# One-hot operands of the routing in tiles of their own, and a new order of issue

## The chip, the cores and the metric

The kernel runs on one core of a Trainium2 chip. The metric is the time on the device of one execution, in microseconds (us), as the median of three runs. One further execution was profiled, and its trace is what is read here.

## The reference, cut to what matters

```python
# 1. attention with random features: 4 batches, 8 heads, 576 tokens, 64 wide, 128 features
q_p, k_p = phi(q_s), phi(k_s)                 # exp(x @ omega.T - ... - rowmax) / sqrt(m)
kv = einsum('bhsm,bhsd->bhmd', k_p, v);  z = sum(k_p, axis=2)
num = einsum('bhsm,bhmd->bhsd', q_p, kv)
den = einsum('bhsm,bhm->bhs', q_p, z)[..., None] + 1e-06
x = num / den                                 # 2304 tokens of 512
# 2. dense layer
h = x @ w_in                                  # 512 -> 1024
solu = h * softmax(h)
x = layernorm(solu) * g_ln @ w_out            # 1024 -> 512
# 3. one expert of 8 for each token
logits = x @ w_gate;  e_idx = argmax(logits);  gate_w = softmax(logits)[e_idx]
eom = sigmoid(x @ w_output_gate)
for e in range(8):
    out[mask] = gate_w[mask] * eom[mask, e] * (relu(x[mask] @ w1[e]) @ w2[e])
```

## The kernel before, in words

The 2304 tokens are 18 tiles of 128. Everything up to the routing is cut into named steps, and one list, ORDER, says in which order they are issued: `kp7` is step `kp` for tile 7. Each engine issues its own instructions strictly in the order of that list; a second list, LOADS, is the order of the loads on SP's queue. A load waits there until the buffer that it takes over is free: `k` and `q` share six, `v` has three.

The steps of a tile: `kp`, `kx`, `ke` (TensorE, VectorE, ScalarE) make the key features, `kv` adds them into a batch's sums; `vc`, `vt`, `vd`, `vz`, `vy` carry a finished batch's sums into SBUF tiles `kv` and `zb` by way of `kt` and `zk`. `qp`, `qx`, `qe` make the query features, `qz` (GpSimd, tile `pz`), `qr` (VectorE, tile `rd`) and `qs` (GpSimd) divide, `qta`, `qtb` transpose, `qca`, `qcb` copy and `nx` gives the attention's output, which `xh` and `xl` split into a rounded and a remaining part. `ha`, `hb` are the first dense product in two halves, `hxa`, `hxb`, `he`, `ma`, `mz`, `mb`, `mc`, `md`, `me` the activation and the norm, `ta`, `tb`, `ca`, `cb`, `sa`, `sb` its transposed parts `lth` and `ltl`, and `u`, `l` the second product, 24 products of 256 or 272 columns each, with the logits beside `u`; `ua`, `ub`, `la` take the results out of PSUM and `lo` stores them. `da` to `dl`, `ga` to `gd` turn the weights into two parts (chunks 0 to 7 for the first product, 8 to 15 for the second). `wu7` is seven products that are thrown away.

Routing: tiles come in sets, 0 to 3, 4 to 7, 8 to 11, 12 to 14, 15 and 16, and 17. `ra`, `rb`, `rc`, `rd`, `re`, `rf` work out where each token of a set goes. `rg` makes the one-hot operands `ea` and `er` of a tile on VectorE, and `rh` multiplies them into the table `tab`. `za` finds the largest expert, `zl` and `zm` load its weights into `raw1` and `raw2` through SP, and `wa`, `wb` split two quarters of the first; the other two quarters are split in hooks of the first unit and stand in no list. `zb` and `zg` gather the expert's first 256 tokens from tiles 0 to 14, `zt` transposes them, `zh` and `zs` split them into `xteh` and `xtel`.

After the list comes the first unit: `up` makes eight chunks of hidden features from 256 columns, `hth` on ScalarE and `htl` on VectorE, with hooks between the chunks, for the last set (`rest`) and for `raw2`, and `down` follows, in which `first_item` adds the rest of the table and fetches the remaining tokens of the item; `up` then runs at column 256 with 336 columns. From there on the items follow one another.

SBUF: `ab` and `rt` are pools that live through this part, `att` is the attention's; it is closed at `zl0`, and the pool `c1` with `raw1` and `raw2` takes its place. PSUM has eight banks: four in `big`, two in `sm`, two in `kvp` (`tab` and `places` at last); `psh` and `psy` take over those of `big`.

## Time and profile before

| | us |
|---|---|
| three runs, median (lowest to highest) | 609.11 (607.41 to 609.7) |
| the profiled execution | 607.34 |
| its span, from the first to the last instruction | 605.7 |
| TensorE busy | 587.7 |
| VectorE busy | 356.7 |
| ScalarE busy | 298.1 |
| GpSimd busy | 261.0 |

Busy times are unions, so a matmul that starts while another is under way is not counted twice; matmuls are pipelined, and a busy TensorE may still be waiting between them. PE is TensorE's matmul, PEld its weight load, DVE VectorE, ACT ScalarE, POOL GpSimd, SP the queue that issues most loads. TensorE's granted clock was 0.998 of full speed over the span.

### The profile page before, as it was taken

To read this page: it belongs to the slowest core of one execution; us is meant where nothing else is said; L and a number is where in the kernel's file an instruction comes from. 1 tells how busy PE (TensorE), PEld (TensorE's weight loads), DVE (VectorE), ACT (ScalarE), POOL (GpSimd) and SP (SyncE) were. 2 spreads that over 40 slices of the span, in tenths; PEclk is the share of its full clock that TensorE was granted. 3 is DMA by queue.
4 is the path that set the end of the run, shared out by engine and by line. 5 is a ranking of instruction groups with operands and counts; after the bars stand their busy time and mean duration, and the time that the engine had idled before them with its cause. 6 is when DMAs were issued, how large, how long until landed. Compare 5 with 4: busy or idle time off the path is not lost. (4 is left out here: it accounts for less than half of the span.)

```text
span 605.7 us, 12756 instructions
## 1 busy us (share of the span) xinstructions
PE 587.7 (97%) x5022; PEld 519.6 (86%) x5022; DVE 356.7 (59%) x960; ACT 298.1 (49%) x746; POOL 261.0 (43%) x283
## 2 busy tenths in 40 slices
...
GB/s 320 364 238 171 176 67 77 99 1 86 38 53 19 2 19 18 18 19 1 18 20 202 128 58 64 30 111 300 264 140 26 165 109 140 35 36 11 2 52 30
DMA packets 21721, 56.45 MB, mean 93 GB/s; under 512 B 2596, under 2 KB 3004, under 8 KB 21652
## 3 DMA queue, kind: packets, MB, share of 16 engines
...
q14 instruction: 27, 0.22, 0.1%
q10 hardware_dynamic: 288, 0.13, 0.1%
...
## 5 line engine op out<-in xcount | busy, mean ns | idle before, releaser
L164 PE MATMUL x<-w2h,lth 128*128 128x272 f32 (+1 forms) x288 | 83.4, 290 | 0.0
L164 PE MATMUL x<-w2h,ltl 128*128 128x272 f32 (+1 forms) x288 | 82.1, 285 | 0.6 <-DVE ltl L152 0.6
L164 PE MATMUL x<-w2l,lth 128*128 128x272 f32 (+1 forms) x288 | 81.9, 284 | 0.0
L982 DVE SCALAR_TENSOR_TENSOR htl<-hp,hth 128x296 fp32r<-128x296 f32 (+2 forms) x64 | 29.8, 466 | 75.0 <-ACT hth L981 61.1
L498 POOL TENSOR_TENSOR pz<-qe,zb 128x256 f32<-128x256 f32 (+1 forms) x80 | 62.6, 813 | 19.9 <-ACT qe L391 12.0
L164 PE MATMUL hp<-xth,w1h 128*128 128x296 f32 (+1 forms) x224 | 67.6, 302 | 0.6 <-DVE htl L982 0.6
L164 PE MATMUL hp<-xth,w1l 128*128 128x296 f32 (+1 forms) x224 | 67.7, 302 | 0.0
L164 PE MATMUL hp<-xtl,w1h 128*128 128x296 f32 (+1 forms) x224 | 67.2, 300 | 0.0
L164 PE MATMUL yp<-w2h,hth 128*128 128x512 f32 (+2 forms) x168 | 65.5, 390 | 0.0
L164 PE MATMUL yp<-w2l,hth 128*128 128x512 f32 (+2 forms) x168 | 64.4, 383 | 0.0
L164 PE MATMUL yp<-w2h,htl 128*128 128x512 f32 (+2 forms) x168 | 64.3, 383 | 0.0
L164 PE MATMUL h<-w1h,xth 128*128 128x512 f32 x144 | 59.1, 410 | 0.2
L981 ACT ACTIVATE hth<-hp 128x296 fp32r<-128x296 f32 (+2 forms) x64 | 26.7, 418 | 64.2 <-PE hp L164 63.1
L152 DVE TENSOR_TENSOR xtl<-xT,xth 128x512 fp32r<-128x512 f32 (+1 forms) x36 | 23.9, 665 | 58.1 <-ACT xth L885 42.1
L164 PE MATMUL h<-w1l,xth 128*128 128x512 f32 x144 | 57.1, 396 | 0.3 <-DVE w1l L152 0.3
L600 POOL TENSOR_SCALAR s<-s,st 128x1024 f32<-128x1024 f32 x18 | 21.7, 1206 | 82.4 <-DVE st L596 52.9
L164 PE MATMUL h<-w1h,xtl 128*128 128x512 f32 x144 | 57.0, 396 | 0.0
L164 PEld LDWEIGHTS x<-w2h,ltl 128*128 128x128 f32 x288 | 54.2, 188 | 0.9 <-DVE ltl L152 0.9
L164 PEld LDWEIGHTS x<-w2h,lth 128*128 128x128 f32 x288 | 54.2, 188 | 0.7 <-issue 0.2
L164 PEld LDWEIGHTS x<-w2l,lth 128*128 128x128 f32 x288 | 54.3, 188 | 0.5
L1007 POOL DMA_INDIRECT out_y<-y,idxs x20 | 20.1, 1003 | 77.3 <-ACT y L1006 69.6
L512 POOL TENSOR_TENSOR qe<-qe,rd 128x256 f32<-128x256 f32 x72 | 44.1, 644 | 9.2 <-DVE rd L505 9.2
...
## 6 DMA issues: line engine op xcount, KB each, us to landing
raw<-in_w POOLq DMA_DIRECT2D x12, 1024.0 KB
...
raw<-in_w SPq DMA_DIRECT2D x4, 1024.0 KB, 5.6
```

The costliest lines, as they stand in the source:

```text
L152: return eng.tensor_tensor(out=out_, in0=a, in1=hi.bitcast(F32), op=ALU.subtract)
L164: return in_turn(nc.tensor.matmul(ps, **kw))
L498: nc.gpsimd.tensor_tensor(out=pz[r0:r1, hs], in0=of["qe", t][r0:r1, hs], in1=of["zb", b][r0:r1, hs], op=ALU.mult)
L512: nc.gpsimd.tensor_tensor(out=e3[:, hs], in0=e3[:, hs], in1=rd[:, hs].to_broadcast([P, HS, M]), op=ALU.mult)
L600: nc.gpsimd.tensor_scalar(out=s, in0=s, scalar1=st[:, 10:11], scalar2=st[:, 11:12], op0=ALU.mult, op1=ALU.add)
L981: act = nc.scalar.activation(out=hi, in_=ps[:, 0:n], func=AF.Relu)
L982: dve = nc.vector.scalar_tensor_tensor(out=lo, in0=ps[:, 0:n], scalar=0.0, in1=hi.bitcast(F32), op0=ALU.max, op1=ALU.subtract)
L1007: nc.gpsimd.indirect_dma_start(out=out, out_offset=bass.IndirectOffsetOnAxis(ap=idxs[0:k, col:col + 1], axis=0), in_=y, in_offset=None, bo ...
```

## The change

- `ea` and `er` no longer borrow the buffers of `ft` (two) and `df` (four) of the attention's pool, or the pool `c1` after it closed. They have tiles of their own: `ea` two buffers, `er` one buffer in `rt` for tiles 0 to 14; for tiles 15 to 17 both have two in `c1`.
- `kv`, `pz` and `rd` move from the attention's pool to `ab`; `zk` holds one batch at a time, in one buffer, instead of all four.
- `rg15` and `rg16` leave the list. They are issued on VectorE after the first unit's first `htl`, and `rest` after its second; the splits of `raw2` come two chunks later.
- `zt` takes its bank from `big` instead of `sm`.
- `up` uses the banks of `kvp` beside those of `psh` also for the first item's second part.
- LOADS and ORDER are new. The same steps stand in ORDER, but for `rg15`, `rg16` and the `wu`, which sum to 33 instead of 30.

`issue_after` makes the instructions of its block that run on the same engine follow the given one in that engine's queue.

```diff
 LOADS = [(x[0], int(x[1:])) for x in """
-    k8 w9 k3 w10 k6 k0 v0 w2 c0 k1 v1 w1 w6 k2 v2 k10 k4 c1 q1 k7 w5 w0 v3 k5 q0 w11 v4 k9 w3 k11 v5 k12 v7 w4 v8 k13
-    w8 v6 q2 w7 v10 k15 q5 v9 k14 v11 q4 q6 v12 q13 v13 w15 q8 v15 k17 v14 q16 k16 v16 v17 q3 q10 w14 q7 w13 w12 q9
-    q14 q15 q11 q12 q17
+    k0 w10 k1 w9 k8 c0 k2 w2 w1 k6 v0 k4 v1 q0 k10 k3 w6 k5 v3 v2 w5 w0 k7 v4 c1 w4 q1 v7 v5 w11 v6 k9 q5 v8 k11 q2 v9
+    w3 v10 v11 k12 k15 k13 k17 q8 v13 w8 k14 v12 q3 w7 q4 k16 v14 v15 q16 v16 q12 w15 q7 w14 v17 q6 q13 w12 w13 q9 q11
+    q17 q10 q15 q14
 """.split()]
 ORDER = """
-    da9 wu7 kp8 kx8 ke8 wu3 kp3 db9 dc9 dd9 wu6 kp0 kx3 de9 df9 da10 db10 ke3 wu7 kp1 da2 dc10 kx0 ke0 dd10 de10 df10
-    kx1 dp9 dg9 wu2 ga1 gb1 dh9 wu3 kp6 kv0 da1 dp10 db1 ke1 kx6 dc1 db2 dc2 ke6 dl9 wu2 kp2 kx2 dg10 da6 ga2 gb2 dd2
-    dd1 gc1 ke2 de2 df2 dh10 db6 kv1 kp4 kx4 dc6 dp2 dh2 dl10 kv2 ke4 dd6 kp5 kx5 zc0 kv3 da11 de6 kp10 ke5 kx10 de1
-    df1 db11 dp1 kv4 vc0 qp1 qx1 ke10 qe1 kw4 qp0 dl2 dc11 kv5 dh1 df6 dp6 qx0 qe0 kp7 dd11 da5 dl1 gc2 gx2 de11 df11
-    kx7 db5 dc5 vz0 vy0 dh6 kv6 ke7 dd5 de5 da7 kp9 kx9 dp11 ke9 dl6 qz0 qr0 kv7 kv8 gx1 dg11 df5 vt0 dh11 dl11 vc1
...
-    gb6 qe8 qs6 nx7 xh7 md1 me1 md0 qp9 qx9 mz5 ha4 xh3 qe9 xl3 dc13 dd13 de12 df12 qta6 de13 gy7 mb5 gd7 xl7 hb4 qca6
-    qtb6 ta5 qcb6 dh14 ca5 hxa4 hxb4 dp12 dg12 gc6 df13 gx6 he4 nx6 xh6 sa5 dh12 ga4 gy6 gd6 ma4 ha3 dp13 dg13 ga5 mz2
-    dh8 dh13 tb5 mb2 xl6 gb4 gb5 hxa3 gc4 gx4 gc5 gx5 dl8 dl12 ta2 ca2 sa2 gy5 gy4 gd4 vc3 cb5 vz3 hb3 dl13 gd5 hxb3
-    qz8 dl14 u0 qr8 mc2 me0 sb5 he3 ma3 tb2 l0 cb2 mc5 md5 qs8 sb2 vy3 qta8 mz3 ub0 qtb8 mz4 qp11 qx11 qca8 qcb8 qp10
...
-    md10 me10 mb12 mc12 rg5 sb10 u10 l10 mb13 ub10 ra2 rc2 he16 ma16 rb2 re2 mz16 ua10 rh4 za0 qtb17 zl0 rg6 rh5 qcb17
-    tb14 nx17 ha15 hb15 rg7 xh17 rd2 xl17 ha17 cb14 sb14 hxa15 u14 me14 lo9 hxb15 he15 la10 ma15 rf2 mz15 ub14 lo10
-    mb15 rh6 mb16 md12 mc15 ta13 ca13 tb13 cb13 sa13 sb13 ta12 ca12 sa12 l14 ua14 la14 ta15 rh7 ca15 hb17 rg8 rh8 wa0
-    sa15 wa1 hxa17 mc16 hxb17 he17 ma17 mz17 ta16 ca16 mc13 md13 lo14 rg10 zm0 u13 me13 ub13 tb15 tb12 cb12 sa16 cb15
-    tb16 ua13 cb16 mb17 me12 sb12 u12 ub12 ua12 l13 ra3 ta17 rb3 tb17 la13 rg9 rh9 rc3 rd3 l12 la12 rf3 sb16 ca17 u16
-    mc17 re3 md15 me15 md16 lo12 me16 lo13 rh10 wb0 cb17 sb17 sb15 u15 rg11 rh11 ub16 rg12 sa17 md17 rh12 rg13 ub15
-    ua16 wb1 ua15 l15 ra4 rc4 l16 rd4 la15 lo15 rh13 rg14 rh14 zb0 rf4 zg1 zg0 rb4 u17 me17 la16 lo16 re4 ub17 ra5 l17
-    ua17 rg16 la17 rg15 zt0 zt1 zh0 zh1 zs0 zs1 lo17
+    da10 wu7 kp0 kx0 ke0 da9 db10 dc10 dd10 wu3 kp1 kx1 db9 ke1 wu6 kp8 kx8 ke8 dc9 de10 df10 dp10 da2 wu6 kp2 kx2 ke2
+    wu4 kp6 dd9 kv0 kx6 ke6 db2 de9 dc2 kp4 da1 wu4 kp3 kv1 df9 kx4 ke4 dd2 dg10 kx3 db1 dc1 de2 df2 dp9 dg9 ke3 kp5
+    kx5 dh9 wu2 ga2 gb2 dd1 dl9 de1 dh10 df1 kv2 kp10 dl10 kx10 ke5 wu1 ga1 dp2 dh2 dl2 kv3 kv4 da6 db6 da5 db5 dc6
+    gb1 qp0 dc5 dd6 da4 vc0 de6 df6 ke10 dp1 dh1 gc1 qx0 kw4 kv5 qe0 db4 dc4 gc2 dd5 gx2 dl1 de5 kp7 dp6 dh6 kx7 vz0
+    vy0 dl6 zc0 da0 db0 qp1 ke7 qx1 qe1 da11 df5 qz0 kv6 kv7 qr0 kp9 vt0 vd0 dc0 kx9 dp5 dd0 qp5 gy2 qs0 qx5 gx1 ke9
+    qe5 db11 kv8 vc1 vz1 kp11 qta0 qca0 dd4 de0 df0 dp0 qtb0 qcb0 qp2 dc11 kx11 dd11 de11 ke11 dh0 qx2 nx0 vy1 qe2
...
+    gc0 gx7 qs7 gx0 he5 ma5 tb0 cb0 nx3 sb0 qta7 qca7 xh3 xl3 gy0 ga6 gb6 qp9 qx9 da13 db13 qtb7 vz2 dc13 dd13 qcb7
+    ha4 qe9 dl8 qs6 qta6 qca6 de13 df13 gd0 hxa4 dh15 qtb6 qcb6 gy7 gd7 da12 qp8 qx8 qe8 vc3 dp13 dg13 db12 dc12 mz2
+    nx7 dd12 de12 vy2 vz3 dl15 nx6 xh6 xl6 hb4 hxb4 mb2 xh7 xl7 dh14 ga5 gb5 dl14 mc2 ha3 hb3 df12 he4 gc6 gx6 gc5 gx5
+    qz8 ma4 ha6 hxa3 hxb3 he3 dp12 qr8 gy5 dg12 dh13 ma3 ga4 dh12 dl12 ta2 tb2 gb4 me1 qs8 qta8 gd5 gy6 gc4 ca2 sa2
...
+    lo8 ub8 nx15 nx17 xh17 rh5 xl17 hb16 cb10 sb10 rg6 rh6 md12 hxb16 xh15 tb13 xl15 mb14 cb13 sb13 me10 mc14 me12 rg7
+    he16 ma16 mz16 mb16 ta12 u10 ub10 ra2 ua10 rc2 rd2 rf2 ca12 ta14 tb14 l10 ca14 cb14 sa14 la10 sb14 ha15 hxa15 hb15
+    hxb15 ta16 mc16 rb2 md16 rh7 mc13 md13 l14 he15 ma15 me13 tb12 re2 za0 lo10 ha17 mz15 u14 sa12 rg8 rh8 rg9 md14
+    zl0 ca16 hxa17 cb12 sb12 me14 ub14 ua14 la14 lo14 hb17 hxb17 he17 u13 ua13 ma17 mz17 sa16 mb15 ta15 mc15 rh9 rg10
+    ca15 md15 u12 tb16 rh10 ub13 mb17 tb15 l13 ub12 ra3 rb3 mc17 sa15 ua12 cb15 sb15 rg11 md17 me17 la13 zm0 ta17 rc3
+    rd3 rf3 re3 wa0 me15 cb16 sb16 rh11 l12 la12 u15 me16 rg12 rh12 lo13 ub15 rg13 wa1 tb17 ca17 cb17 sb17 sa17 ua15
+    u16 ub16 ra4 lo12 rh13 l15 ua16 rg14 rh14 zb0 wb0 rc4 l16 la15 rd4 zg1 zg0 lo15 wb1 la16 rb4 u17 re4 rf4 ub17 ua17
+    ra5 l17 la17 zt0 lo17 zt1 zh0 zs0 zh1 lo16 zs1
 """.split()]
@@ -352,8 +352,7 @@
 
 
 
-        kvs = ap.tile([P, B, H, D], F32, name="kv")
-        zk = ap.tile([P, B, 2, M], F32, name="zk")
+        kvs = pool.tile([P, B, H, D], F32, name="kv")
         raws = {}
 
         def load_tok(kind, t):
@@ -452,10 +451,11 @@
 
 
         def vc(b):
+            zk = of["zk", b] = ap.tile([P, 2, M], F32, tag="zk", name=f"zk{b}", bufs=1)
             kt = of["kt", b] = ap.tile([P, 2, 2 * M], F32, tag="kt", name=f"kt{b}", bufs=1)
             for g, ps in enumerate(kv_ps.pop(b)):
                 nc.scalar.copy(out=kt[:, g, :], in_=ps[:, 0:2 * M])
-                nc.scalar.copy(out=zk[:, b, g, :], in_=ps[:, 2 * M:3 * M])
+                nc.scalar.copy(out=zk[:, g, :], in_=ps[:, 2 * M:3 * M])
 
         def vt(b):
             kt, pss = of.pop(("kt", b)), []
@@ -473,13 +473,14 @@
 
 
         def vz(b):
+            zk = of.pop(("zk", b))
             if b:
-                nc.sync.dma_start(out=zd[b - 1:b].rearrange("o (g i m) -> (o i) g m", g=2, i=4), in_=zk[0:P:32, b])
+                nc.sync.dma_start(out=zd[b - 1:b].rearrange("o (g i m) -> (o i) g m", g=2, i=4), in_=zk[0:P:32])
                 return
             of["zp", b] = pss = [half_bank(f"zp{b}_{n}").rearrange("p (i g m) -> p i g m", i=2, g=2) for n in range(2)]
             for i in (0, 2, 1, 3):
                 rows = slice(i // 2 * D, i // 2 * D + D)
-                mm(pss[i // 2][:, i % 2], lhsT=ident[rows, 32 * i:32 * i + 1].to_broadcast([D, P]), rhs=zk[rows, b], start=True, stop=True)
+                mm(pss[i // 2][:, i % 2], lhsT=ident[rows, 32 * i:32 * i + 1].to_broadcast([D, P]), rhs=zk[rows], start=True, stop=True)
 
         def vy(b):
             zb = of["zb", b] = ap.tile([P, H, M], F32, tag="zb", name=f"zb{b}", bufs=2)
@@ -491,14 +492,14 @@
 
 
         def qz(t):
-            pz = of["pz", t] = ap.tile([P, H, M], F32, tag="pz", name=f"pz{t}", bufs=1)
+            pz = of["pz", t] = pool.tile([P, H, M], F32, tag="pz", name=f"pz{t}", bufs=1)
             for b, r0, r1, _, _ in segments(t):
                 for h in range(0, H, HS):
                     hs = slice(h, h + HS)
                     nc.gpsimd.tensor_tensor(out=pz[r0:r1, hs], in0=of["qe", t][r0:r1, hs], in1=of["zb", b][r0:r1, hs], op=ALU.mult)
 
         def qr(t):
-            rd = of["rd", t] = ap.tile([P, H, 1], F32, tag="rd", name=f"rd{t}", bufs=2)
+            rd = of["rd", t] = pool.tile([P, H, 1], F32, tag="rd", name=f"rd{t}", bufs=2)
             r2 = rd[:, :, 0]
             nc.vector.reduce_sum(out=r2, in_=of.pop(("pz", t)), axis=AX.X)
             nc.vector.tensor_scalar(out=r2, in0=r2, scalar1=1e-6 * M, scalar2=None, op0=ALU.add)
@@ -694,7 +695,6 @@
                 V.memset(keep[n], 1.0)
                 V.memset(keep[n][:, :, 0:1], 0.0)
 
-        hp, EA, ER = ap, ("ft", 2), ("df", DF)
         count = [None]
         d0, e0 = r("d0", [P, E]), r("e0", [P, 1])
         first = {}
@@ -810,9 +810,9 @@
 
             i = next(i for i, (a, z) in enumerate(SETS) if a <= t < z)
             k, d = t - SETS[i][0], of["r", i]
-            ea = hp.tile([P, 512], F32R, tag=EA[0], name=f"ea{t}", bufs=EA[1])[:, 0:P]
+            ea = (cx if t >= TA else rt).tile([P, P], F32R, tag="ea", name=f"ea{t}", bufs=2)
             V.tensor_scalar(out=ea, in0=row[:, 0:P], scalar1=d["flo"][:, k:k + 1], scalar2=None, op0=ALU.is_equal)
-            er = hp.tile([P, 512], F32R, tag=ER[0], name=f"er{t}", bufs=ER[1])[:, 0:3 * NR].rearrange("p (i n) -> p i n", i=3)
+            er = (cx if t >= TA else rt).tile([P, 3, NR], F32R, tag="er", name=f"er{t}", bufs=2 if t >= TA else 1)
             V.scalar_tensor_tensor(out=er, in0=row.unsqueeze(1).to_broadcast([P, 3, NR]), scalar=d["col"][:, k:k + 1],
                                    in1=tsc[:, t, :].unsqueeze(2).to_broadcast([P, 3, NR]), op0=ALU.is_equal, op1=ALU.mult)
             of["hot", t] = ea, er
@@ -905,7 +905,7 @@
             gather(first["xge"], j, idxe[:, j:j + 1], TA * P)
 
         def zt(j):
-            ps = of["xTe", j] = sm.tile([P, NPAIR, P], F32, tag="sm", name=f"xTe_{j}")
+            ps = of["xTe", j] = half_bank(f"xTe_{j}").rearrange("p (c m) -> p c m", c=NPAIR)
             for c in range(NPAIR):
                 transpose(ps[:, c, :], first["xge"][:, j, c * P:(c + 1) * P])
 
@@ -947,14 +947,13 @@
                      za=za, zc=zc, wu=warm, zl=zl, zm=zm, zb=zb, zg=zg, zt=zt, zh=zh, zs=zs, wa=wa, wb=wb, wc=wc)
         in_order(begin, 0)
         for what in ORDER:
-            if not first and (what == "zl0" or what.startswith("rg") and int(what[2:]) >= TE):
+            if not first and (what == "zl0" or what.startswith("rg") and int(what[2:]) >= TA):
                 att.close()
                 cx = ctx.enter_context(tc.tile_pool(name="c1", bufs=1, side="right", reuse_waits="tile"))
                 raw1 = first["raw1"] = cx.tile([P, NPAIR, EF], F32, name="raw1")
                 raw2 = first["raw2"] = cx.tile([P, EF // P, DM], F32, name="raw2")
                 first["xge"] = cx.tile([P, CA, DM], F32, name="xge")
                 xte = first["xte"] = [cx.tile([P, NPAIR, CA * P], F32R, name=f"xte{k}") for k in "hl"]
-                hp, EA, ER = cx, ("ea", 2), ("er", 2)
             name = what.rstrip("0123456789")
             in_order(steps[name], int(what[len(name):]))
             if what == f"vc{B - 1}":
@@ -970,7 +969,7 @@
     def up(i, xt, ht, at, n, between={}):
 
         for f in range(EF // P):
-            more = i and f % 4 > 1
+            more = (i or at) and f % 4 > 1
             ps = (kvp if more else psh).tile([P, 512], F32, tag=f"kv{f % 2}" if more else "psh", name=f"hp{i}_{f}_{at}")
             for hook in between.get(f, ()):
                 hook()
@@ -1026,9 +1025,16 @@
     last = []
     got = cp.tile([P, 3, NR], F32, name="got")
     V.tensor_copy(out=got, in_=table)
-    hooks = {2: [lambda: rest(len(SETS) - 1)], 4: [lambda: [rh(t) for t in range(TA, TA + 2)]]}
+    
+    def behind(*steps):
+        with tc.issue_after(done_up[1]):
+            for step in steps:
+                step()
+
+    hooks = {1: [lambda: behind(lambda: rg(TA), lambda: rg(TA + 1))], 2: [lambda: behind(lambda: rest(len(SETS) - 1))],
+             4: [lambda: [rh(t) for t in range(TA, TA + 2)]]}
     for c in range(4):
-        hooks.setdefault(1 + c, []).append(lambda c=c: split_behind(raw2, w2h, w2l, (c,), ()))
+        hooks.setdefault(3+c, []).append(lambda c=c: split_behind(raw2, w2h, w2l, (c,), ()))
     for c in (2, 3):
         hooks.setdefault(c - 2, []).insert(0, lambda c=c: split_expert(raw1, w1h, w1l, (c,), ()))
     up(0, xte, ht, 0, CA * P, hooks)
```

## Rows read from the trace of the kernel before

**Rows 1.** The page: busy us, share of the span, instructions

```profile
PE 587.7 (97%) x5022; PEld 519.6 (86%) x5022; DVE 356.7 (59%) x960; ACT 298.1 (49%) x746; POOL 261.0 (43%) x283
```

**Rows 2.** Windows, all engines: busy us and instructions in each stretch

```profile
core 0: us, PE busy (x) PEld busy (x) DVE busy (x) ACT busy (x) POOL busy (x), PEclk, DMA share, GB/s
...
0.00:10.00 10.00, 8.75 (x68) 8.00 (x70) 4.18 (x10) 5.07 (x13) 0.19 (x4) 1.00 0.78 279
...
10.00:150.00 140.00, 135.22 (x1947) 111.87 (x1945) 134.34 (x281) 114.19 (x348) 96.55 (x104) 1.00 0.45 150
...
150.00:360.00 210.00, 208.18 (x1587) 189.81 (x1587) 136.73 (x451) 99.46 (x249) 76.00 (x108) 1.00 0.13 45
...
360.00:380.00 20.00, 17.61 (x138) 16.34 (x137) 15.90 (x72) 8.22 (x16) 2.89 (x3) 1.00 0.21 67
...
460.00:470.00 10.00, 10.00 (x44) 8.10 (x44) 3.50 (x3) 3.74 (x6) 5.34 (x4) 1.00 0.22 61
...
590.00:605.70 15.70, 8.47 (x61) 7.66 (x59) 0.00 (x0) 1.63 (x3) 1.90 (x2) 0.91 0.12 41
```

**Rows 3.** Timeline of TensorE: start, us; in brackets idle before and its releaser

```profile
368.56 1.21 PE L168 MATMUL xTe<-ident,xge 128*128 128x128 f32 x8
...
370.44 0.38 PE L164 MATMUL hp<-xteh,w1h 128*128 128x256 f32 x1 [0.68 <-ACT xteh L913]
...
372.53 0.38 PE L164 MATMUL hp<-xtel,w1h 128*128 128x256 f32 x1 [1.70 <-DVE xtel L152]
```

**Rows 4.** Timeline of VectorE, the last 9 us before `xtel` is done

```profile
362.28 0.17 DVE L842 TENSOR_TENSOR pick<-tab,d 128x16 f32<-128x16 f32 x1 [1.48 <-PE tab L164]
...
368.40 0.17 DVE L724 TENSOR_TENSOR oh<-desc,em 128x8 f32<-128x8 f32 x1
...
369.19 0.16 DVE L798 TENSOR_REDUCE gw<-dl 128x1 f32<-128x8 f32 x1 [0.62 <-ACT dl L753]
...
370.35 0.71 DVE L816 SCALAR_TENSOR_TENSOR er<-nums,col,tsc 128x480 fp32r<-128x480 f32 x1
...
371.20 1.28 DVE L152 TENSOR_TENSOR xtel<-xTe,xteh 128x512 fp32r<-128x512 f32 x2
```

**Rows 5.** Timeline of ScalarE, the same stretch

```profile
369.22 1.17 ACT L913 CAST xteh<-xTe 128x512 fp32r<-128x512 f32 x2
```

**Rows 6.** Timeline of VectorE in the first unit

```profile
374.54 0.43 DVE L982 SCALAR_TENSOR_TENSOR htl<-hp,hth 128x256 fp32r<-128x256 f32 x1 [0.17 <-ACT hth L981]
...
375.49 1.23 DVE L152 TENSOR_TENSOR w2l<-raw,w2h 128x1024 fp32r<-128x1024 f32 x1 [0.53 <-ACT w2h L155]
...
384.18 0.72 DVE L816 SCALAR_TENSOR_TENSOR er<-nums,col,tsc 128x480 fp32r<-128x480 f32 x1
...
387.15 0.66 DVE L1052 TENSOR_TENSOR got<-got,tab 128x480 f32<-128x480 f32 x1 [0.76 <-PE tab L164]
```

**Rows 7.** Windows, products of `x` alone: columns as in rows 2, without POOL

```profile
362.60:368.40 5.80, 5.80 (x48) 5.74 (x48) 0.23 (x1) 0.47 (x1) 1.00 0.46 136
```

**Rows 8.** Timeline of TensorE in the first item

```profile
386.73 0.38 PE L164 MATMUL tab<-er,ea 128*128 128x480 f32 x1
...
402.31 0.42 PE L164 MATMUL hp<-xth,w1h 128*128 128x336 f32 x1 [0.58 <-DVE htl L982]
```

**Rows 9.** Groups by line on VectorE: busy us, mean ns of one

```profile
L152 DVE TENSOR_TENSOR w2l<-f,w2h 128x512 fp32r<-128x512 f32 x8 | 7.1, 899 | 0.0
...
L152 DVE TENSOR_TENSOR ltl<-lT,lth 128x512 fp32r<-128x512 f32 x36 | 23.7, 681 | 14.2 <-ACT lth L628 14.2
```

**Rows 10.** Timeline of SP in the head

```profile
36.71 0.33 SPq L364 DMA_DIRECT2D v<-in_v  x1
```

**Rows 11.** Timeline of TensorE in the head

```profile
41.65 0.64 PE L164 MATMUL kv<-ke,v 128*32 128x128 f32 x16 [1.61 <-DMA v<-in_v]
```

**Rows 12.** DMA issues: KB each, median us to landing

```profile
raw<-in_w SPq DMA_DIRECT2D x4, 1024.0 KB, 5.6
```

**Rows 13.** Windows, the 70 us before the hand-over, columns as in rows 2

```profile
298.00:368.00 70.00, 68.90 (x514) 64.77 (x513) 51.77 (x209) 31.44 (x68) 16.29 (x20) 1.00 0.28 98
```

More of the change, by code (lines that the diff above doesn't have):

```diff
@@ L96 @@
-    mb3 ua0 la0 md2 qz9 qr9 l1 qe11 qz11 ta3 qx10 qs9 me2 qr11 qs11 u1 ub1 ua1 ha6 ca3 sa3 u2 qe10 ub2 qta11 qz10 qr10
-    mc3 md3 la1 lo1 ua2 tb3 cb3 qca11 qtb11 qcb11 mb4 mc4 sb3 l2 la2 lo2 me3 qp12 qx12 qe12 nx8 xh8 lo0 hxa6 hb6 hxb6
-    he6 qta9 ma6 xl8 qtb9 u3 qca9 qcb9 qz12 mz6 ta4 ca4 sa4 ua3 ub3 qp14 qx14 nx11 qe14 nx9 xh9 ra0 qp16 qx16 rc0 xl9
-    ha7 mb6 qe16 hb7 rb0 tb4 xh11 cb4 hxa7 hxb7 he7 l3 ha8 qs10 la3 lo3 ma7 mz7 mc6 sb4 qta10 qtb10 hb8 qca10 qcb10
-    re0 mb7 ta7 mc7 tb7 ca7 cb7 nx10 qr12 qs12 sa7 sb7 rd0 ha9 xh10 hb9 xl10 hxa8 qz14 hxb8 he8 hxa9 me5 xl11 u5 qr14
```

42 lines of the change are left out of this document (23 added, 19 removed).

## The prediction

> **What bounds the kernel now.** I read the page first, then the windows, then TensorE's waits, then the timelines of the two places that the change touches. The page has TensorE busy in 97% of the span [rows 1]: 587.7 of 605.7 us, 18 idle. The windows say where the idle time lies [rows 2]: 1.3 us in the first 10, 4.8 from 10 to 150, 1.8 from 150 to 360, 2.4 from 360 to 380, and 7.2 in the last stretch, where the last rows are scattered, which the change leaves alone. So a new order of the same products can take back idle time in two places: the head, and the hand-over from routing to the first expert.
>
> In the head "busy" hides waiting. From 10 to 150 VectorE is busy 134.3 of 140 us, while weight loads fill 111.9; from 150 to 360 VectorE falls to 65% and weight loads rise to 90% [rows 2]. The head goes at VectorE's pace, and what counts there is how much VectorE work a list puts ahead of the product that waits for it. The Trainium skill ("Trainium Kernel Development and Optimization", Performance Expectations) calls matmul busy time a bad measure of how near the limit a kernel is and wants LDWEIGHTS busy share instead. By busy time a better list could win 4.8 us from 10 to 150; by that rule's measure the 28 us without a weight load there. The windows side with the rule, and the second rival below goes past what idle time alone allows.
>
> TensorE's own waits are short: 1.61 us for a `v` [rows 11], 0.68 for `xteh` and 1.70 for `xtel` [rows 3], 0.58 for an `htl` [rows 8].
>
> **Hand-over.** After the last product of tile 17 the eight transposes of `xTe` run from 368.56 to 369.77; one product starts at 370.44, after ScalarE's `xteh`, and the next at 372.53, after VectorE's `xtel` [rows 3]. VectorE had waited 0.62 us for an exponential of the last set, then made `ea` and `er` of tiles 15 and 16 (`rg15`, `rg16`: 369.33 to about 370.98) and three small steps of the last set, and only at 371.20 the two `xtel` [rows 4]. ScalarE's two `xteh` were done at 369.22 + 1.17 = 370.39 [rows 5]. The change takes `rg15`, `rg16` and the last set's steps from VectorE's queue ahead of `zs0`, and gives `zt` a bank of its own, so `zt1` no longer waits for `la17`. What is late next is ScalarE: the second `xteh` at 370.3 to 370.4, then one more `xtel` at 0.64 (half of 1.28), so TensorE resumes at 371.0 instead of 372.53: **-1.5**. Bounds: the new list puts both `wb` (1.23 us for a like quarter [rows 6]) behind `zb0`, where VectorE's chain `zb0`, `rf4`, `re4`, `ub17`, `ra5` was just in time; against it stand `l16`, `u17` and `l17`, 24 products each at 5.80/48 = 0.121 us [rows 7], 8.7 us. The chain took from 362.28 to 368.57 [rows 4], 6.3, and with 2.4 more 8.7: a tie, and up to one `wb` may be lost. So -1.6 to -0.3.
>
> **First unit of the expert.** What left VectorE's queue comes back here. Before, from the end of `xtel` (372.48) to the end of `er` of tile 17 (384.90) passed 12.4 us [rows 4, 6]; `rh17` stood on TensorE at 386.73 [rows 8], 14.2 us after the resumption, and VectorE then idled 0.76 for it. Now VectorE may not begin `rg15` before the first `htl`, which started 2.06 us after `xtel` ended, nor the last set before the second. It takes in 1.65 more (`rg15`, `rg16`), and some 1.4 of small steps that filled the wait ahead of that `htl` come later; 0.7 of its idle time goes, as the quarters of `w2l` start two chunks later. That is 14.8, or 13.6 if one `w2l` (1.22) falls behind `er`, against 14.2: 0.6 early to 0.6 late. Queued behind are the `htl`, for whose bank TensorE waits two chunks later. I take **+0.4**; bounds 0 and +3.0, the latter if all four `w2l` come first and the two `w1l` quarters that are in no list (2.44) fall here as well, since `raw1` now loads later: 14.8 + 2.4 - 14.2.
>
> **Second half of the first item.** `up` now uses four banks in place of two for it. TensorE's wait for `htl` at 402.31 was 0.58 [rows 8]; a third chunk no longer needs the first chunk's `htl`. **-0.6**, between 0 and twice that; the two banks held `tab` and `places`, read last at 387.15 [rows 6], long before.
>
> **Head: new lists.** I compare the two lists at `qta8`, in both near the last product that VectorE's total holds up. Ahead of its `qr8` the old list has, and the new one has not, `dl12`, `dl13`, `sa2`, `sa5`, three `gd`, `mz5` and `md0`: 2 x 0.90 + 2 x 0.68 [rows 9], and fourteen short ones near 0.16 [rows 4], together 5.4 us of VectorE. Ahead of `qta8` it also has on TensorE `u0`, `l0` (2.9 each) and 1.5 of short turns; the new one has `ha6`, 12 products of 512 columns at 10/44 = 0.227 [rows 2], 2.7. So the product comes 5.4 earlier and leaves 4.6 more to do: -0.8 at best, 0 at worst, since other products wait too: **-0.3**. Three more units of `wu` (66 instructions for 60) fall where TensorE waits anyway; with no wait there they would cost 6 x 0.11 = 0.7.
>
> The loads share SP's queue, where a `v` waits for one of three buffers. Before, `v6` was issued at 36.71, once `kv5` was done, and `kv6` stood until 41.65 [rows 10, 11]. The new LOADS puts `v7` (which needs `kv3` done) in front of `v5`, and `v8` behind `kv7`: two tight places again, as `v6` and `v9` were. VectorE was busy through it, so 0.
>
> **At nothing.** `kvs`, `pz` and `rd` below the attention's pool and `zk` for one batch at a time: same instructions; `vc` waits for the `vz` before it, several tiles earlier. `zl0` comes later on SP, some 19 us of products, and holds back the stores queued behind; a `raw` load landed 5.6 us (median) after its issue [rows 12], and `hb17`, `u13`, `u12`, `l13` and turns, over 11 us, stand between `zl0` and `wa0`. If not covered, the excess is paid once.
>
> **Sum.** -1.5 + 0.4 - 0.6 - 0.3 = -2.0. The profiled execution took 607.34 (605.7 span, 1.64 around it), so 605.3; the median of the runs shown, 609.11, lies 1.77 above it, so on that scale **607.1**. 0.5% is 3.05 us, about what a measurement of this kernel can tell from no change: below 606.06 is faster, above 612.16 slower.
>
> **Rivals.** *Second: the lists win more in the head.* VectorE's idle time there is 5.8 in the first 10 us and 5.7 from 10 to 150 [rows 2]; a third of it, 3.6, would come off whole, because the head goes at VectorE's pace: 603.5. For it: the old list's stops for `v`; against: the same two kinds of stop in the new one.
>
> *Third: VectorE is late in the first unit*, at its bound of +3.0 in place of +0.4: 609.7. For it: VectorE has 15.9 of 20 us busy from 360 to 380 [rows 2]. Against: some of the `w2l` are not needed until the second product group.
>
> *Fourth, slower: one `er` buffer below tile 15 where there were four.* `rg(t+1)` must wait until `rh(t)` has run, and behind it in VectorE's queue stand `ltl` and `lg` that the next products need. Ten of the 14 waits fall from 298 to 368, where VectorE idles 18.2 us [rows 13]. A wait can last one group of 24 products, 2.9: ten make 29, 10.8 beyond its idle time. It decides from 1.8 us a wait; halfway to the bound it costs 5.4: 612.5. For it: VectorE already stood 1.5 for TensorE's `tab` at 362.28 [rows 4]. Against: in the list `rg13` and `rg14` stand behind a `ub` that waits for almost the same product. The Trainium skill ("Trainium Kernel Development and Optimization", Best Practices) asks for double buffers, though there for overlapping DMA with compute; its advice speaks against this edit, and no row before shows one buffer.
>
> **Chances.** Forecast 0.44 (own range 605.2 to 609.1), second 0.26, third 0.12, fourth 0.18. Faster: all of the second and 0.09 of the forecast, 0.35. Slower: 0.15 of the fourth. Same: 0.50. The range runs from 603.0, a little below the second, to 612.5.
>
> **What would show it.** `xtel` straight behind `xteh`, and the stop ahead of the second `hp` at most 0.8; no `htl` wait at the third chunk of 336 columns; the VectorE end of `er` of tile 17 against `rh17`; VectorE's idle time to 150 us within 1.5 of 11.5. The prediction is wrong if the head moves by more than 3 us either way, or VectorE stands at `er` for `tab` over 10 us.

## The result, and the profile after

| | us |
|---|---|
| after, median of four runs (lowest to highest) | 603.38 (602.98 to 604.27) |
| before, median of four runs | 608.5 (607.41 to 609.7) |
| ratio, 95% interval | 0.9909 (0.9885 to 0.9934) |
| profiled execution, its span | 602.98, 601.3 |

The kernel became 0.9% faster, where 0.3% was forecast (607.1 for 609.11); 603.38 lies below the forecast's own range, which began at 605.2. The profiled executions lie 4.36 us apart, twice the -2.0 of the sum.

The page and the windows of the kernel after, to be laid beside [rows 1, 2]:

```profile
PE 585.9 (97%) x5028; PEld 519.9 (86%) x5028; DVE 358.8 (60%) x960; ACT 298.5 (50%) x746; POOL 263.1 (44%) x283
```

```profile
core 0: us, PE busy (x) PEld busy (x) DVE busy (x) ACT busy (x) POOL busy (x), PEclk, DMA share, GB/s
0.00:10.00 10.00, 8.82 (x76) 8.11 (x78) 4.42 (x11) 5.31 (x14) 0.19 (x4) 1.00 0.77 273
10.00:150.00 140.00, 135.20 (x1943) 111.74 (x1940) 133.68 (x278) 113.08 (x345) 98.12 (x104) 1.00 0.44 150
150.00:360.00 210.00, 209.07 (x1608) 192.02 (x1607) 141.47 (x458) 100.67 (x250) 78.65 (x109) 1.00 0.13 46
360.00:380.00 20.00, 18.81 (x151) 18.02 (x150) 16.36 (x78) 8.86 (x17) 1.18 (x2) 1.00 0.17 54
```

In the head VectorE and the weight loads are busy as before (133.68 and 111.74 us for 134.34 and 111.87). From 150 to 360 TensorE issues 1608 products where it issued 1587, and in the next 20 us 151 for 138. That points at a gain in a stretch that the sum had no term for.

Busy time alone doesn't size it. The table counts TensorE's lost time: for each product the time from the end of the one before to its own end, less what that form on these operands takes when nothing disturbs it (the mean of its undisturbed ones in all these traces); `wu` counts as lost. The last two columns are from TensorE's end to that of the span, and the span.

| kernel | to 160 | 160 to 360 | 360 to 390 | from 390 | behind | span |
|---|---|---|---|---|---|---|
| before | 49.9 | 7.1 | 4.1 | 0.9 | 7.2 | 605.7 |
| after | 50.0 | 4.9 | 2.6 | 0.0 | 7.4 | 601.3 |
| e1, old lists | 49.2 | 19.6 | 5.2 | 2.2 | 8.4 | 621.0 |
| e2, before with new lists | 50.8 | 5.3 | 5.3 | 0.9 | 7.5 | 606.1 |
| e3, two banks | 50.6 | 4.9 | 2.6 | 0.9 | 7.2 | 602.6 |
| e4, one-hots ahead | 50.1 | 4.9 | 4.7 | 0.2 | 7.2 | 603.6 |
| e5, old lists and buffers | 49.8 | 6.9 | 3.6 | 0.0 | 7.2 | 604.1 |
| e8, parts behind `xtel` | 50.0 | 3.9 | 4.2 | 0.5 | 8.3 | 603.3 |
| e9, parts on GpSimd | 50.6 | 9.6 | 3.5 | 0.0 | 7.5 | 607.5 |
| e11, early `w2l` | 53.7 | 5.6 | 3.7 | 0.1 | 7.2 | 606.8 |
| e12, before, shifted | 51.8 | 13.8 | 5.0 | 1.2 | 7.5 | 615.7 |
| e13, parts in the list | 50.6 | 3.8 | 2.5 | 0.0 | 7.5 | 600.8 |
| e14, the same in before | 49.5 | 6.6 | 6.0 | 0.9 | 7.7 | 607.2 |

Only differences between kernels are read from this table: the losses themselves depend on which products are taken as undisturbed. From 160 to 360 us the four profiles of before (the last experiment has three more) lie within 0.2 us of one another, to 160 us within 2. So half of the 4.4 us is won in the middle.

The view of TensorE's waits from 160 to 360 us, first of the kernel before, then of the one after (us in total, times, longest):

```profile
PE x L164 <- DVE ltl L152: 0.6, 1, 0.6
PE xT L164 <- DVE st L593: 0.5, 1, 0.5
PE lT L168 <- DVE s L587: 0.5, 1, 0.5
```

```profile
PE tab L164 <- DVE er L816: 0.9, 1, 0.9
```

Three stops went and one came. With the slower products behind each, the three cost 2.3 us and the one 1.2; the other 1.1 of the 2.2 is spread over small losses, most of them where one kind of product follows another.

TensorE, ScalarE and VectorE at the hand-over and in the first unit, timelines of the kernel after, beside [rows 3 to 6, 8]:

```profile
366.24 1.03 PE L168 MATMUL xTe<-ident,xge 128*128 128x128 f32 x8
368.01 0.39 PE L164 MATMUL hp<-xteh,w1h 128*128 128x256 f32 x1 [0.73 <-ACT xteh L913]
368.84 0.39 PE L164 MATMUL hp<-xtel,w1h 128*128 128x256 f32 x1 [0.45 <-DVE xtel L152]
...
383.04 0.38 PE L164 MATMUL tab<-er,ea 128*128 128x480 f32 x1
```

```profile
366.88 1.07 ACT L913 CAST xteh<-xTe 128x512 fp32r<-128x512 f32 x2
```

```profile
367.50 1.29 DVE L152 TENSOR_TENSOR xtel<-xTe,xteh 128x512 fp32r<-128x512 f32 x2 [1.32 <-ACT xteh L913]
...
375.28 1.22 DVE L152 TENSOR_TENSOR w2l<-raw,w2h 128x1024 fp32r<-128x1024 f32 x1
...
381.85 0.70 DVE L816 SCALAR_TENSOR_TENSOR er<-nums,col,tsc 128x480 fp32r<-128x480 f32 x1
```

VectorE now waits for ScalarE's first `xteh` (1.32), and the two `xtel` follow it. From the transposes' start to the second `hp` pass 2.60 us for 3.97. From there to `rh17` pass 14.20 us, to the hundredth the time of before. The 96 products of 336 columns stand without a wait.

**The clock in the medians.** In the profile of before the granted clock was 1.00 behind the hand-over [rows 2], but it isn't in every execution. Of the 75 runs of before beside the experiments 27 had a mean clock of 0.997 or more and took 606.25 to 609.76 us (median 607.8); 40 had 0.994 or less and took 607.51 to 612.46 (median 610.2). The groups overlap: the mean also counts a lower clock behind TensorE's last product (0.75 in the last 5.7 us of the profile of before, where TensorE is busy 0.00), and other losses vary too. The four runs after have 0.997 or 0.998. Three more profiles of before (last experiment) show where it falls.

### The profile page after: what moved, and what is told of

It reads as the page before. It is cut to its first block, busy times and chain, and to the rows that moved or that the text cites. A ratio compares the mean times of both kernels' runs of the same rounds, so it can differ in the third digit from the quotient of the medians.

```text
span 601.3 us, 12772 instructions
## 1 busy us (share of the span) xinstructions
PE 585.9 (97%) x5028; PEld 519.9 (86%) x5028; DVE 358.8 (60%) x960; ACT 298.5 (50%) x746; POOL 263.1 (44%) x283
## 5 line engine op out<-in xcount | busy, mean ns | idle before, releaser
L1005 ACT ACTIVATE y<-yp,scs 128x512 f32<-128x512 f32 (+2 forms) x21 | 14.0, 667 | 66.8 <-PE yp L164 64.0
```

The costliest lines, as they stand in the source:

```text
L1005: nc.scalar.activation(out=y[:, d:d + width], in_=ps, func=AF.Copy, scale=scs[0:k, col:col + 1])
```

## Experiments

Each was timed in five rounds against before, on the same chip, but for the last three (one execution each). Medians of before there lay at 608.8 to 609.4; TensorE's lost time of most is in the table above. A difference to the kernel after is one between medians of separate sets of runs, so a few tenths of a us of it mean nothing.

**The lists alone, and all but the lists.** e2 puts the new LOADS and ORDER into the kernel before (with `rg15` and `rg16` beside `la17`); e5 puts the old lists into the kernel after, with `ea` and `er` in the old buffers; e1 the same with the new buffers, where `rg` steps had to move behind the `rh` of the tile before, as there is one `er`.

```diff
 LOADS = [(x[0], int(x[1:])) for x in """
-    k0 w10 k1 w9 k8 c0 k2 w2 w1 k6 v0 k4 v1 q0 k10 k3 w6 k5 v3 v2 w5 w0 k7 v4 c1 w4 q1 v7 v5 w11 v6 k9 q5 v8 k11 q2 v9
+    k8 w9 k3 w10 k6 k0 v0 w2 c0 k1 v1 w1 w6 k2 v2 k10 k4 c1 q1 k7 w5 w0 v3 k5 q0 w11 v4 k9 w3 k11 v5 k12 v7 w4 v8 k13
...
-            er = (cx if t >= TA else rt).tile([P, 3, NR], F32R, tag="er", name=f"er{t}", bufs=2 if t >= TA else 1)
+            er = hp.tile([P, 512], F32R, tag=ER[0], name=f"er{t}", bufs=ER[1])[:, 0:3 * NR].rearrange("p (i n) -> p i n", i=3)
```

> The changed kernel with the LOADS and ORDER of before; only the steps rg are shifted in them so that each follows the rh before it, as one er buffer demands. Theory one (the traces: the hand-over gives 1.5 us, the four banks 0.85, the lists 2.2 between 160 and 360 us, the head nothing): 2.4 us below before, about 606; TensorE's time lost up to 160 us unchanged at 50.0, up to 360 us 7 more as before. Rival, the buffers and banks make the gain in the middle whatever the list: 4.3 to 5 below before, about 603.5. Rival, the lists make all of it: as before, 608.5.

> The kernel before with the LOADS and ORDER of the change, rg15 and rg16 put beside la17 as before. Theory one: 2.2 us below before, about 606.3, all of it between 160 and 360 us; the stops of 0.7 and 1.7 at the first unit and the 0.58 at its second half stay. Rival, the lists need the new buffers: no gain, 608.5 or slower. Rival, the lists make all of it: 603.5.

> The changed kernel with the old lists, as in e1, but ea and er in the buffers of before (four er below tile 12), and the old order of rg. Theory: e1's 14 us came from the single er buffer in lists not made for it, and all else of the change keeps its 2.4 us: 2.2 to 2.6 below before, about 606.3; no stop of 4 us at tab or behind it. Rival, the moved tiles (kv, pz, rd, zk) cost in the old lists: above 610.

e2 took 608.1 us, ratio 0.9991 (0.9975 to 1.0007), by the time its first rival: no gain. e5 took 607.29, 0.9966 (0.9948 to 0.9985), a little less of a gain than its theory said; e1 622.36, 1.0222 (1.0193 to 1.0251), slower than all it had in view. The two halves of the change, 0.7 and 2.0 us under their medians of before, don't add up to the whole. But from 160 to 360 us the loss follows the list and not the buffers: 5.3 for e2 and 4.9 after, 6.9 for e5 and 7.1 before. To 160 us e2 and e5 lie 1 us apart, and before itself took 49.9 and, in the three profiles of the last experiment, 48.6 to 50.5. What e2 won in the middle it lost in the head and behind the hand-over: its stop was still 1.70 us, and the granted clock fell to 0.53 behind it (372 to 375 us); all its 12 runs have a mean clock of 0.990 to 0.995. LOADS and ORDER always went in together, so which of the two wins the middle wasn't tried. e1 shows what a single `er` does with a list that isn't made for it; the timeline of its VectorE:

```profile
293.51 0.72 DVE L816 SCALAR_TENSOR_TENSOR er<-nums,col,tsc 128x480 fp32r<-128x480 f32 x1 [6.13 <-PE tab L164]
```

VectorE stood 6.13 us for `tab`; behind this `er` it made an `st` for which ScalarE had by then stood 8.68 us, and TensorE stood 4.01 us for ScalarE's `xo`, which came behind that. But the moved `rg` steps were in e1 too, so e12 has them in the kernel before, with its four buffers:

```diff
...
-    md8 hb13 rd1 qr15 mz10 mb10 ha12 ta10 hxa13 hxb13 he13 ca10 xh14 xl14 rb1 sa10 rh1 me8 l4 qs15 qta15 la4 u8 rg3
...
+    rd1 qr15 mz10 mb10 ha12 ta10 hxa13 hxb13 he13 ca10 xh14 xl14 rb1 sa10 rh1 rg2 me8 l4 qs15 qta15 la4 u8 ma13 u9
...
```

> The kernel before, whose one-hot steps stand in its list as in the first experiment (each behind the reductions of the tile before it), with its four buffers as they were. Nothing is left out. Theory one (the 14 us that the first experiment lost against the old buffers are the single buffer's): within 3 us of the time before, 608 to 612. Rival (they are the shifted steps', whatever the buffers): 616 or more.

617.49 us, 1.0136 (1.0112 to 1.016): the rival, mostly. TensorE's timeline:

```profile
317.25 0.77 PE L164 MATMUL tab<-er,ea 128*128 128x480 f32 x1 [4.05 <-DVE er L816]
```

So of e1's 15.1 us over e5 the shifted steps are worth some 8.4 (617.49 less 609.1), one stop of 4.05 us at `tab` among them, which e1 has too, and the single buffer the rest, about 7, with the stop of 4.01. These prices are of stop and clock together: the granted clock fell at each of the stops (0.66 from 298 to 303 us and 0.58 from 318 to 326 in e1, 0.53 from 316 to 323 in e12). In e1 alone I had put all of it down to the buffer.

**Old and new list in one.** e6 has the old list in the kernel after up to `l1`, then the new; e7 the new one in the kernel before up to `u1`, then the old; of e7:

```diff
 ORDER = """
-    da9 wu7 kp8 kx8 ke8 wu3 kp3 db9 dc9 dd9 wu6 kp0 kx3 de9 df9 da10 db10 ke3 wu7 kp1 da2 dc10 kx0 ke0 dd10 de10 df10
+    da10 wu7 kp0 kx0 ke0 da9 db10 dc10 dd10 wu3 kp1 kx1 db9 ke1 wu6 kp8 kx8 ke8 dc9 de10 df10 dp10 da2 wu6 kp2 kx2 ke2
...
```

> The changed kernel with the old lists up to l1 (about 160 us) and the new ones from there. Theory: the head is worth the same in both lists and the lists' 2.2 us are made behind 160 us: within 0.8 us of the changed kernel, about 603.5. Rival, the new head leaves the later part better placed: 2.2 us slower than the changed kernel, about 605.6.

> The kernel before with the new lists up to u1 and the old ones from there. Theory: as before within 0.8 us, TensorE's time lost from 160 to 360 us at 7 as before. Rival, the new head brings the gain: 2.2 below before.

e6 took 607.02 us, 0.9971 (0.9953 to 0.9989), e7 613.01, 1.007 (1.0047 to 1.0093), both slower than they had in view. Neither is a clean half: where the lists meet, from 160 to 180 us, they lose some 4 us (e7 in one stop of 2.3 for ScalarE's `xo`). Outside the seam, from 180 to 360, e6 lost 4.8 as after (4.7), e7 6.5 as before (6.5), and both heads 49.7. That agrees with e2 and e5, no more.

**Edits of the hand-over and the first unit, undone one by one in the kernel after.** e4 puts `rg15` and `rg16` back beside `la17`; e10 puts `zt` back into `sm`; e11 lets `w2l` start two chunks earlier; e3 gives the second half two banks.

```diff
-    ra5 l17 la17 zt0 lo17 zt1 zh0 zs0 zh1 lo16 zs1
+    ra5 l17 rg16 la17 rg15 zt0 lo17 zt1 zh0 zs0 zh1 lo16 zs1
...
-            ps = of["xTe", j] = half_bank(f"xTe_{j}").rearrange("p (c m) -> p c m", c=NPAIR)
+            ps = of["xTe", j] = sm.tile([P, NPAIR, P], F32, tag="sm", name=f"xTe_{j}")
...
-        hooks.setdefault(3+c, []).append(lambda c=c: split_behind(raw2, w2h, w2l, (c,), ()))
+        hooks.setdefault(1 + c, []).append(lambda c=c: split_behind(raw2, w2h, w2l, (c,), ()))
...
-            more = (i or at) and f % 4 > 1
+            more = i and f % 4 > 1
```

> The changed kernel with rg15 and rg16 in the list again, beside la17, and the last set free to go early. Theory one: TensorE's stop ahead of the second hp is back at 1.6 to 1.9 us from 0.45, 1.2 to 1.5 slower than the changed kernel, 2.8 to 3.1 below before. Rival, the work that it takes from VectorE in the first unit is worth as much there: as the changed kernel, 4.3 below before.

> The kernel after, with the transposes of the gathered rows in the banks of the second layer's products, as before the change; lists and everything else as after. Nothing is left out. Theory one (the half bank lets them go ahead of the last eviction of those products, 366.44 to 366.91): the second block's four transposes wait for that eviction, the splits come 0.4 to 0.9 us later, and the time is 0.4 to 0.9 us over that after, about 604.0. Rival (the hand-over's 1.5 us come from the place of the last one-hots alone, a bank is free anyway): the time after within 0.3 us.

> The kernel after, with the splits of the second weight matrix again two chunks earlier in the first unit (from the second chunk on in place of the fourth). Nothing is left out. Theory one (in the first unit the order on VectorE decides, four parts of 1.2 us ahead of er of tile 17 make rh17 and what follows it late): 0.5 to 1.5 us over the time after, about 604.4, with a wait for VectorE at tab or htl between 374 and 386. Rival (there is slack for both orders): the time after within 0.3 us.

> The changed kernel, but the first item's second part uses two banks again. Theory one: 0.85 us slower than the changed kernel, so 3.5 below before by the span, and a wait of 0.5 to 0.6 for htl at the third chunk of 336 columns. Rival, the earlier hand-over frees VectorE in time and the wait is gone anyway: as the changed kernel, 4.3 below before.

- e4: 605.13 us, 0.9942 (0.9923 to 0.9961), 1.75 over after: about the time of theory one, but not its mechanism. The stops grew only from 0.73 and 0.45 to 0.82 and 0.82, not to 1.6 or more. Of the 2.1 us more that its trace loses from 360 to 390 us, 0.46 are these stops; the rest are slower products behind them, where the granted clock fell. The window of e4 with it (columns as above):

```profile
369.50:373.50 4.00, 4.00 (x23) 4.00 (x24) 2.03 (x11) 0.59 (x2) 0.00 (x0) 0.63 0.00 0
```

So the one-hots' place alone doesn't make the stop of 1.70 us of before. e2 has it with the same late one-hots beside the old bank, the old buffers and the early `w2l`, and there VectorE also stands for an exponential of the last set, `dl`, ahead of the one-hots, as it did before (0.62 in [rows 4]); in e4 that step comes behind them, without a wait. Which of the other edits moves it wasn't tried. VectorE's timeline of e2:

```profile
368.24 0.16 DVE L798 TENSOR_REDUCE gw<-dl 128x1 f32<-128x8 f32 x1 [1.07 <-ACT dl L753]
```

- e10: 603.52, 0.9908 (0.9886 to 0.9931). The rival's time: with all else of the change in place, the transposes' new bank is worth nothing. That the whole gain is that of the one-hots' place, as the rival has it, is not shown (e4).
- e11: 605.2, 0.9926 (0.9905 to 0.9947), 1.8 over after, as theory one or a little beyond: at 378.88 TensorE waits 0.77 us for an `htl` that stands behind a `w2l`. By the trace, 1.1 of it lies from 360 to 390 us. The trace also has 3.7 more in the head, where the granted clock was 0.51 from 33 to 40 us; it is of the slowest of seven runs, 3.3 us over their median.
- e3: 604.45, 0.9932 (0.9907 to 0.9957), 1.07 over after, as theory one: the wait for `htl` is back, with 0.56 us idle and 0.9 lost, as before.

**The stop at 339.62.** VectorE after, ahead of it:

```profile
334.93 1.23 DVE L152 TENSOR_TENSOR w1l<-raw,w1h 128x1024 fp32r<-128x1024 f32 x1
...
336.15 1.21 DVE L152 TENSOR_TENSOR w1l<-raw,w1h 128x1024 fp32r<-128x1024 f32 x1
...
338.86 0.70 DVE L816 SCALAR_TENSOR_TENSOR er<-nums,col,tsc 128x480 fp32r<-128x480 f32 x1
```

The two quarters of `w1l` that no list places run as soon as `raw1` is there, ahead of the `er` that TensorE waits for. e8 queues them behind the last `xtel`, e9 gives them to GpSimd, e13 puts them into the list, and e14 puts them into the list of before, both behind `rg14`. The edits of e8, e9 and e13, each without the two hooks' own splits:

```diff
+    def behind_split(c):
+        with tc.issue_after(first["zs"]):
+            split_expert(raw1, w1h, w1l, (c,), ())
...
-        hooks.setdefault(c - 2, []).insert(0, lambda c=c: split_expert(raw1, w1h, w1l, (c,), ()))
+        hooks.setdefault(c - 2, []).insert(0, lambda c=c: behind_split(c))
```

```diff
+    def pooled_split(c):
+        upper_quarter(raw1, w1h, c)
+        with tc.issue_after(moved["me"]):
+            lower_quarter(nc.gpsimd, raw1, w1h, w1l, c)
```

```diff
-    zl0 ca16 hxa17 cb12 sb12 me14 ub14 ua14 la14 lo14 hb17 hxb17 he17 u13 ua13 ma17 mz17 sa16 mb15 ta15 mc15 rh9 rg10
+    zl0 ca16 hxa17 cb12 sb12 me14 ub14 ua14 la14 lo14 hb17 hxb17 he17 wa2 wa3 u13 ua13 ma17 mz17 sa16 mb15 ta15 mc15 rh9 rg10
...
-    rd3 rf3 re3 wa0 me15 cb16 sb16 rh11 l12 la12 u15 me16 rg12 rh12 lo13 ub15 rg13 wa1 tb17 ca17 cb17 sb17 sa17 ua15
-    u16 ub16 ra4 lo12 rh13 l15 ua16 rg14 rh14 zb0 wb0 rc4 l16 la15 rd4 zg1 zg0 lo15 wb1 la16 rb4 u17 re4 rf4 ub17 ua17
+    rd3 rf3 re3 wa0 me15 cb16 sb16 rh11 l12 la12 u15 me16 rg12 rh12 lo13 ub15 rg13 wa1 tb17 ca17 cb17 sb17 wb2 sa17 ua15
+    u16 ub16 ra4 lo12 rh13 l15 ua16 rg14 wb3 rh14 zb0 wb0 rc4 l16 la15 rd4 zg1 zg0 lo15 wb1 la16 rb4 u17 re4 rf4 ub17 ua17
```

> The changed kernel, but the two quarters of w1l that stand in no list are queued on VectorE behind the last xtel; in the changed kernel they run at 335 to 337.3 us ahead of an ltl and an er, and TensorE stops 0.93 us at that er. Theory: the stop goes, 0.9 us below the changed kernel, 602.5. Rival, the 2.4 us of VectorE come back in the first unit, as waits for htl or at rh17: as the changed kernel or up to 1.5 slower.

> The kernel after, with the two lower parts of the first weight matrix that no list places (1.23 and 1.21 us on VectorE at 334.93 and 336.15) on GpSimd, behind its last small power of the last tiles, where its rows show it idle from 345.05 to 358.18; the third such part takes 2.85 us there later on. Nothing is left out. Theory one (TensorE's 0.93 us stop at 339.62 is VectorE's, which is late for tab by those two parts): the stop goes and nothing takes its place, since VectorE's first unit gets no work in return: 0.6 to 1.2 us under the time after, about 602.4 us. Rival: VectorE only gives the slack back, at the next reduction or in the first unit, or its neighbour GpSimd slows it from 345 to 351: the time after within 0.4 us, 603 to 604.

> The kernel after, with the two parts of the first weight matrix that no list placed put into the list: on VectorE one behind the low halves of tile 17 (its idle 1.18 us at 352.90) and one behind the one-hots of tile 14, on ScalarE where they were. Nothing is left out. Theory one (the 0.93 us stop at 339.62 is theirs, and VectorE's idle time around 353 and 356 takes them): 0.6 to 1.2 us under the time after, about 602.5 us. Rival (VectorE has no room to give: the pick of the gathered rows comes 0.6 us later and with it the hand-over, or a one-hot): 603 to 604.5, with a new stop between 350 and 370.

> The kernel before, with the same two parts put into its list on VectorE, both behind the one-hots of tile 14, and on ScalarE where they were. Nothing is left out. Theory one (the parts at 334.03 to 336.39 make lT and x late at 336.61 and 340.07, 0.67 and 0.92 us, and a good part of the gain between 160 and 360 us is where such work fell): 1.0 to 1.6 us under the time before. Rival (the order of the listed steps makes these stops, or the 1.48 us idle ahead of the pick is no room): within 0.6 us of the time before.

- e8: 604.68 us, 0.993 (0.9908 to 0.9953), 1.3 over after. The stop is gone, but in the first unit TensorE waits 0.31 for an `htl` and 0.82 for `er` of tile 17: the rival.
- e9: 610.0, 1.0007 (0.9991 to 1.0024), outside both expectations. Timelines of its VectorE, GpSimd and TensorE:

```profile
344.55 2.35 DVE L805 CAST gwh<-gw 128x3 fp32r<-128x3 f32 x1
346.94 2.33 DVE L806 COPY tsc<-gwh 128x3 f32<-128x3 f32 x1
```

```profile
344.49 4.75 POOL L152 TENSOR_TENSOR w1l<-raw,w1h 128x1024 fp32r<-128x1024 f32 x2
```

```profile
353.68 0.64 PE L164 MATMUL tab<-er,ea 128*128 128x480 f32 x1 [3.96 <-DVE er L816]
```

Two conversions of three numbers a partition, 0.17 us each in their other places, took 2.35 and 2.33, as long as one GpSimd part each, and TensorE stood 3.96 us for the `er` behind them; the granted clock was 0.66 from 353 to 358 us.
- e13: 602.24 (601.43 to 602.67), 0.9878 (0.9847 to 0.9909). Theory one: from 160 to 360 us the view of TensorE's waits is empty, and 1.1 us less than after is lost there, with nothing in its place. It is faster than before, and its slowest run is below the fastest after, though those two were timed apart and their ratios' intervals overlap.
- e14: 609.29, 1.0007 (0.9983 to 1.0031). The rival: before's stop for `ltl` stays (0.7), and only 0.5 of the 7.1 went, so it is the order of its listed steps, not these parts, that makes most of the difference to after. The hand-over lost 1.9 us more, with a stop of 1.93 and the granted clock at 0.50 behind it (374 to 376 us).

**Before once more, three profiles.**

> The kernel before, unchanged, one more profile, to see where the granted clock falls when its mean is 0.995 or less. Theory one (the stop of 1.70 us at 370.37 to 372.53 sometimes lets the clock fall, as the stop of that size did in the second experiment): 609 us or more, with products at half pace in the 2 to 3 us behind that stop and nowhere else from 20 us on. Rival (the clock falls in the loading of the first 20 to 50 us, which the change does not touch): half pace there, and the full pace behind the stop.

> As the run before it, of the same kernel: theory one expects a mean granted clock under 0.995 to come with half pace behind the stop at 370 to 372.5 us, the rival with half pace in the first 50 us; with a mean of 0.997 or more neither shows, and the time is about 607.5 us.

> As the two runs before it, of the same kernel: 607.5 us at a mean granted clock of 0.997 or more, 609 us or more under it, with half pace behind the stop at 370 to 372.5 us by theory one, in the first 50 us by the rival.

They took 609.11, 607.43 and 610.49 us. Windows of the second and the third behind the stop:

```profile
372.00:376.00 4.00, 4.00 (x25) 4.00 (x23) 2.50 (x8) 1.93 (x5) 0.00 (x0) 0.58 0.00 0
```

```profile
372.00:376.00 4.00, 3.07 (x14) 3.07 (x15) 2.43 (x11) 0.52 (x3) 0.00 (x0) 0.51 0.00 0
```

Behind the same stop of 1.70 us TensorE ran at half pace for some microseconds, at the lower of its two levels, and the losses from 360 to 390 us were 5.2 and 6.4 where the profile of before has 4.1. In the first 50 us the granted clock was 1.00 in all three. So the place is theory one's, but its times are not: the second took 607.43 at a mean of 0.994, as its head lost least (48.6), and the first kept its clock behind the stop (1.00, lost 4.1) and still took 609.11, 1.0 of it from a longer stretch behind TensorE's end (8.2). Nor is the rival's place ruled out for other executions: the granted clock fell in the head in e11, and it was 0.66 from 42 to 47 us in e12.

## Why the prediction was wrong, point by point

- **Head: 0 for -0.3.** 50.0 lost for 49.9; VectorE's idle time to 150 us is 11.9 for 11.5, inside the bound that was set. Profiles of before alone differ by more (48.6 to 50.5), so 0 and -0.3 can't be told apart. The 28 us without a weight load that were seen as room from 10 to 150 us are still there (140.00 less 111.74).
- **The step that failed is "Head: new lists", with the first paragraph's "two places".** There it is said that a new order can win in the head and at the hand-over, and the 1.8 us from 150 to 360 us, in the same list of idle time, get no term. "Head: new lists" then compared the two lists at one place, `qta8`, and let that stand for all of them. From 160 to 360 us 2.2 us were won. Part was in sight: three waits that cost 2.3 with what follows them. By e2 and e5, and outside their seam by e6 and e7, the gain follows the lists, and the buffers alone win nothing. Which moved steps did it, and how the 1.1 us of small losses went, wasn't tried. The signs that were set for being wrong watched the head and `er`, and neither shows this.
- **Hand-over: -1.5, as forecast.** 1.5 us less are lost from 360 to 390 us, 1.37 of it won by the second `hp`. `xtel` stood straight behind `xteh`, and the stop ahead of that `hp` was 0.45. It doesn't hang on the new lists: with the old ones (e5) 2.88 us pass from the transposes' start to the second `hp`, for 3.97 before and 2.60 after. The bank of `zt` alone had no part in it (e10), and no `wb` was lost: VectorE idled 1.32 us ahead of `xtel`. With the one-hots back in the list, and the last set free to go early, 0.46 us of stop come back (e4); VectorE's wait for the last set's `dl`, ahead of the one-hots before, does not, and which edit removes it is open. What the term left out is the clock: in two of four profiles of before it fell behind this stop, at a price of 1.1 and 2.3 us. That can account for the distance between 4.4 us on the profiles and 5.1 on the medians, but the head varies as much, so the share isn't shown.
- **First unit: 0 for +0.4.** VectorE took 13.76 us from `xtel` to `er` of tile 17, between the 13.6 and 14.8 of its two cases. That it lies near the first is luck: that case has one `w2l` behind `er`, and all four came ahead of it (375.28 to some 381.3), so the working of the other was 1.0 too long. With the old lists (e5) TensorE did stand 0.63 us at `rh17` for that `er`. The two `w1l` quarters, whose fall into this unit was the upper bound, came at 334.93 and cost 1.2 us there instead; e8 shows that here they would have cost at least as much (1.6 us more lost from 360 to 390, 0.5 from there on).
- **Second half: right in kind, -0.9 for -0.6.** The wait is gone and nothing came for it. The term took the idle 0.58; with the slower products behind it a wait of that size costs 0.9 (e3 has 0.9 back).
- **At nothing:** no row after speaks against it; in the list neither ScalarE nor VectorE waited for a `raw`.
- **Rivals.** The second named the lists but the wrong stretch. That its 603.5 came out is luck: the head won nothing, and a third of its 11.5 us is 3.8, not 3.6. The third didn't come, though e11 puts its price, with `w2l` early, at 1.8. The fourth's mechanism is real: 6.13 us at `er` in e1. In the new list VectorE stands for `tab` there once, 0.8 us, as each `rg` follows the `rh` that frees its buffer. The Trainium skill's advice on double buffers ("Trainium Kernel Development and Optimization", Best Practices) decided nothing here: one buffer cost about 7 us in e1's order, and no stop of TensorE that the trace shows in the new one.

On the profile the sum should have read 0 for the head, -2.2 for the middle, -1.5, 0, -0.9 and +0.2 behind TensorE's end: -4.4. It read -2.0, and the middle is nearly all that it lacked.
